# How x reaches the feed-forward layer's channel layout: TensorE transposes, or VectorE block transposes and a trip through memory

## The chip, the core and the metric

The kernel runs on one core of one Trainium2 chip. The metric is the device time of one execution in microseconds. Three runs of the kernel before gave 473.37, 473.84 and 475.94; the median is 473.84.

## What is computed

An mLSTM attention (4 sequences, 8 heads, 768 steps, 40 values a head) makes x of 3072 tokens by 320 channels, and a feed-forward layer (320 to 2048 to 320, with a leaky activation that has a slope of its own for each hidden channel) makes the output of it:

```
m_new = max(f + m, i);  C = exp(f + m - m_new) C + exp(i - m_new) v k^T;  n likewise with k
x = sigmoid(o) * (C q) / max(|n q|, 1)          # 8 heads of 40 side by side: 320 channels
h = x @ w_in;  g = max(h, 0) + alpha * min(h, 0);  out = g @ w_out
```

## The kernel before

The attention is done in its chunked form. A chunk is 128 tokens (n = 0 to 23), with tokens on the partitions; a group g is two chunks (256 tokens), and there are twelve groups (0 to 11). Chunks 0 to 5 (`NDIR = 6`), that is groups 0 to 2, are done in an opening whose order is written out by hand in `ORDER`. From group 3 on one string, `PATTERN`, is unrolled once a group: a name such as `xn.-1` is a step of chunk 2g-1, `X:-1` a step on x of group g-1, `V0<<` an up-step of the feed-forward layer of group g-2. Every engine runs its instructions in exactly the order in which the unrolled names issue them (`pin`), and an engine that waits holds up all that stands behind it. SyncE (SP) issues nearly all DMAs, in the same way: one queue, in order. The DMAs take turns on eight semaphores, so that one waits for the landing of the one issued eight before it.

**x by token.** `gated_steps` (L399) normalizes one chunk: reciprocal of the denominator, times the gate, times the numerator into the tile `xn` (L420, VectorE, 128 tokens by 320 channels). GpSimd then copies channels 256 to 319 a second time behind them (L424), since the third block of channels is used twice, once for each half of `W2`.

**x by channel.** The feed-forward layer's first matmuls need channels on the partitions. `x_steps` (L576) takes two PSUM tiles, has TensorE transpose the six blocks of 128 by 128 (`x_by_channel`, L551), and then splits the result into a rounded part and its rest for exactness: ScalarE copies to `XH` (L565) and `X2` (L568), VectorE subtracts to `XL` (L570) and `X2L` (L573). In `PATTERN` these are X (transposes), xa and xb (the two copies), xd and xe (the two subtractions).

**The feed-forward layer.** A group's eight up-steps (`up_steps`, L687) make 256 hidden channels each by 16 matmuls into a PSUM tile `ph` (L697 to L704; two such tiles take turns), then Relu on ScalarE (L707), the activation's other half on VectorE (L712), a rounded copy `gh` on ScalarE (L721) and the rest `gl` on GpSimd or VectorE (L723). Eight down-steps (L734) of 12 matmuls add up the output, which VectorE copies out (L767). V0 and U0 are the first up-step of a group; V0 is the first reader of the group's `XH` and `XL`.

**Other work on SP that stands close to x.** Two crossbar transposes a chunk bring q and k to channels (L269), four copies shift them (`shifted`, L279 to L282, the first two wait for the crossbar's landing), `state` sends the attention's state to its places (L233, L234, L236), `load_L` brings 512 KB of decays (L119), and `load_gate` (L128) brings six chunks of the output gate, once a sequence. The scratch tile that `state` sends from (tag `qf`) is one of two that `token_parts` also uses (L260), so the second of its GpSimd subtractions waits for the landing of L233 and L234.

Of the kernel before, what the change touches and what calls it, by code (L numbers as in the profile page):

```python
# [8 lines left out]
F32 = mybir.dt.float32  # L9
F32R = mybir.dt.float32r  # L10
# [3 lines left out]
ALU = mybir.AluOpType  # L14
# [3 lines left out]
def kernel(ctx: ExitStack, tc: tile.TileContext, q, k, v, i_gate, f_gate, o_gate, w_in, w_out, alpha, out):  # L18
# [380 lines left out]
    def gated_steps(n, hv):  # L399
        b, c = divmod(n, NC)  # L400
        g, j = divmod(n, GC)
        if j == 0:
            xn_tiles[g] = sb.tile([P, GC, DM + KR], F32, tag="xn", name=f"xn{g}")
        xn = xn_tiles[g]
        r = sb.tile([P, H], F32, tag="r", name=f"r{n}")
        if 0 < c and n < NBF:
            nc.vector.scalar_tensor_tensor(r, hv[:, :, D], 2.0, hv[:, :, D + 1], ALU.max, ALU.max)
        else:
            nc.vector.tensor_scalar(r, hv[:, :, D], 2.0, None, ALU.max)
            nc.vector.tensor_tensor(r, r, hv[:, :, D + 1], ALU.max)  # L410
        nc.vector.reciprocal(r, r)
        yield
        sg = o_tiles[b][:, c]
        rb = r.unsqueeze(2).broadcast_to([P, H, D])
        if b == 0:
            nc.vector.scalar_tensor_tensor(out=sg, in0=sg, scalar=1.0, in1=rb, op0=ALU.add, op1=ALU.mult)
        else:
            nc.gpsimd.tensor_tensor(sg, sg, rb, ALU.mult)
        yield
        (nc.gpsimd if c > 0 and n in XNP else nc.vector).tensor_tensor(  # L420
            xn[:, j, :DM].rearrange("p (h d) -> p h d", d=D), hv[:, :, :D], sg, ALU.mult
        )
# [19 lines left out]
    def late_steps(n):  # L442

        b, c = divmod(n, NC)
        g, j = divmod(n, GC)
        E, pS, Es, got = {}, {}, [None, None], {}

        def decays(par):
            Lb = pre[n] if par == 0 else pre.pop(n)
            E[par] = decays_of(n, par, Lb)  # L450
            if par == 0:
                got["E3"] = late_pool.tile([P, 2, 512], BF16, tag="t", name=f"E3_{n}", bufs=3)
            parts = E[par].bitcast(BF16).rearrange("p (k s) -> p k s", k=2)
# [24 lines left out]
        def add():  # L478
            nc.vector.tensor_tensor(got["T"], got["T"], got["S"], ALU.add)

        def gate():
            got["g"] = gated_steps(n, got["T" if c > 0 else "S"])
            next(got["g"])

        def upd():
            got["u"] = update_steps(n)
            next(got["u"])

        def tok():
            got["t"] = token_parts(n)  # L490
            next(got["t"])

        def val():
            got["v"] = value_parts(n)
            next(got["v"])

        def nxt(k):
            return lambda: got.__setitem__("S", next(got[k]) or got.get("S"))

        st = {}  # L500
        if n >= NDIR + 2:
            st["ld"] = lambda: load_qk(n)
            if j == 0:
                st["lv"] = lambda: load_v(g)
            st["lL"] = lambda: pre.__setitem__(n, load_L(n))
            st["ta"] = tok
            for k in "bcdefghi":
                st["t" + k] = nxt("t")
        if n > NDIR:
            st["sh"] = lambda: shifted(n)  # L510
            st["va"] = val
            for k in "bcd":
                st["v" + k] = nxt("v")
# [24 lines left out]
        st["r"] = gate
        for k in ("og", "xn", "xp"):
            st[k] = nxt("g")  # L540
        return st

    def drain(it):
# [1 line left out]
            pass  # L545

    def x_by_channel(g, j, p1, p2, kts=range(3)):
        xn = xn_tiles[g]
        for kt in kts:
            dst = p1[:, kt * GT :] if kt < 2 else p2  # L550
            nc.tensor.transpose(dst[:, j * P : (j + 1) * P], xn[:, j, kt * P : (kt + 1) * P], ident)  # L551

    def x_tiles_of(g):
        XH = sb.tile([P, 2, GT], F32R, tag="XH", name=f"XH{g}")
        XL = sb.tile([P, 2, GT], F32R, tag="XL", name=f"XL{g}")
        X2 = sb.tile([P, GT], F32R, tag="X2", name=f"X2{g}")
        X2L = sb.tile([P, GT], F32R, tag="X2L", name=f"X2L{g}")
        return XH, XL, X2, X2L

    def split_steps(g, ts, p1, p2, whole=False):  # L560
        if g not in x_tiles:
# [33 lines left out]
    def first_stacks():  # L595
# [40 lines left out]
        U12 fm5 ft5 o5h sc51 wg51 v5 o7d R12 S12 ta5 D10 G11 K11 o6s o6x gr5 og3 gg5 G12 gx5 gg4 D11 K12 D12 i30h i30l  # L636
        gx4 U13 gp5 D02 tp0 do3 U06 o7s gp4 o5l o6j vp0 R13 tp1 g05 S13 G13 N05 K13 o7x o6h D13 vp1 o7j U07 tp2 tp3
        R06 S06 R07 x4 x5 xa5 xd5 D03 D04 D05 S07 o7h o7l G06 K06 o6l D06 xa4 xd4 G07 K07 D07 Z0"""
    PATTERN = """og.-1 ua.0 m1.0 V4<< tf.1 ub.0 vb.1 xn.-1 V5<< tg.1 g2<< m0.0 N2<< vc.1 c1.0 r4<< vb.0 d1.0 xp.-1 th.1 h1.0 ti.1 uc.0
        s4<< ud.0 D2<< ue.0 U6<< g4<< l1.0 g3<< N3<< uf.0 r5<< lG.-1 c0.0 vd.1 X:-1 vc.0 ua.1 lG.2 sh.1 ub.1 s5<< N4<<  # L640
        oa.0 R6<< d0.0 g5<< ug.0 h0.0 l0.0 uc.1 V7<< N5<< xa:-1 vd.0 D3<< D4<< D5<< S6<< ta.2 tb.2 xb:-1 uh.0 lL.2
        y0.0 xd:-1 pi.0 r7<< s7<< G6<< wd.2 tc.2 K6<< ob.0 xe:-1 q0.0 td.2 y1.0 F< q1.0 e0.1 te.2 V0< e1.1 tf.2 g7<<
        ud.1 s0.1 r0< s1.1 V1< m0.1 s0< ui.0 c0.1 tg.2 m1.1 ta.3 c1.1 pt.0 d0.1 N7<< ad.0 D6<< ld.4 V2< D7<< th.2 d1.1
        ue.1 g0< uf.1 tb.3 r1< h0.1 r.0 s1< V3< l0.1 og.0 ug.1 ti.2 uh.1 wd.3 tc.3 h1.1 lv.4 r2< e0.2 xn.0 sh.2 Z<<
        l1.1 td.3 ui.1 pi.1 g1< s2< y0.1 N0< ld.5 xp.0 pt.1 e1.2 q0.1 r3< N1< y1.1 D0< q1.1 D1< s0.2 s1.2 va.3 ad.1
# [258 lines left out]
    def first_group():  # L904
# [398 lines left out]
```

## Time and profile before

| | |
|---|---|
| three runs: lowest, median, highest | 473.37, 473.84, 475.94 us |
| span of the profiled execution, first to last instruction | 474.2 us |
| TensorE matmul busy | 467.8 us, 99% of the span |
| VectorE, ScalarE, GpSimd busy | 308.6, 314.8, 308.4 us (65%, 66%, 65%) |
| x transposes on TensorE (L551) | 72, in 12 groups of six |
| DMA traffic | 61.61 MB, mean 130 GB/s |

The profiled execution has no time of its own beside its span; the span and the runs agree within 0.1% at the median. Times in rows are counted from the start of the span. PE is TensorE's matmuls, PEld its weight loads, DVE is VectorE, ACT ScalarE, POOL GpSimd, SPq the queue of SyncE. Matmuls overlap in the pipeline, so the row of one is longer than the distance to the next one's start.

### The profile page before, as it was taken

What the parts mean: (1) busy time and instruction counts of PE and PEld (TensorE: products, weight loads), DVE (VectorE), ACT (ScalarE), POOL (GpSimd) and SP (SyncE); (2) the same over time, 40 slices, a digit from 0 to 9 for tenths busy, and PEclk for the clock granted to TensorE, in tenths of its full rate; (3) what the DMA queues carried; (4) which work ended last, traced back from release to release, by engine and by line L of the source; (5) the groups of instructions that cost most, each with busy time, mean ns of one, the idle gap of its engine ahead of it and who ended that gap; (6) DMA issues with size and microseconds to landing.
All of it is one profiled execution on the core that took longest, in us unless ns stands there. A gap on an engine that the chain in (4) does not pass through costs nothing.

```text
span 474.2 us, 11834 instructions
## 1 busy us (share of the span) xinstructions
PE 467.8 (99%) x4442; PEld 454.9 (96%) x4442; DVE 308.6 (65%) x664; ACT 314.8 (66%) x716; POOL 308.4 (65%) x395
## 2 busy tenths in 40 slices
PE   8999999999999999999999999999999999999997
PEld 6899989999999999999999999999999999999997
DVE  3768988757776676676676676676676676663321
ACT  4969888766858659558658659558658658424322
POOL 8531674864788688578788688578788686334231
PEclk9959999999999999999999999999999999999999
DMA  9978994968784665768963784699784442000000
GB/s 186 207 175 225 267 217 121 209 130 167 160 156 116 133 150 117 129 150 174 148 148 108 111 169 117 126 148 184 147 129 114 94 113 61 1 28 1 29 2 28
DMA packets 173923, 61.61 MB, mean 130 GB/s; under 512 B 140154, under 2 KB 166122, under 8 KB 173866
## 3 DMA queue, kind: packets, MB, share of 16 engines
q1 hardware_dynamic: 173786, 60.75, 61.3%
q8 instruction: 35, 0.57, 0.6%
q14 instruction: 22, 0.18, 0.1%
q10 hardware_dynamic: 80, 0.11, 0.1%
HBM read 36.90 MB, written 4.03 MB: 86 GB/s over the span
## 4 chain that ended last, share of the span: by engine, by line
PE 89%; DVE 5%; POOL 2%; ACT 2%; issue 1%; POOLq 0%; DVEq 0%; ACTq 0%
PE po L734 35%; PE ph L697 5%; PE ph L703 4%; PE ph L700 4%; PE ph L698 4%; PE ph L699 4%; PE ph L702 4%; PE ph L704 4%; PE ph L701 4%; PE pH L361 4%; PE pS L462 3%; PE pH L322 2%; PE p L551 2%; PE pu L183 2%; PE pS L1033 1%; PE pI L386 1%
## 5 line engine op out<-in xcount | busy, mean ns | idle before, releaser
L723 POOL TENSOR_TENSOR gl<-g,gh 128x512 fp32r<-128x512 f32 x77 | 100.2, 1303 | 41.2 <-ACT gh L721 34.2
L734 PE MATMUL po<-OH,gh 128*128 128x320 f32 x368 | 110.7, 312 | 0.0
L734 PE MATMUL po<-OL,gh 128*128 128x320 f32 x368 | 109.4, 309 | 0.0
L707 ACT ACTIVATE g<-ph 128x512 f32<-128x512 f32 x96 | 57.2, 597 | 75.9 <-PE ph L704 71.8
L712 DVE SCALAR_TENSOR_TENSOR g<-g,oma,ph 128x256 f32<-128x256 f32 x156 | 67.0, 471 | 36.1 <-ACT g L707 36.0
L734 PEld LDWEIGHTS po<-OL,gh 128*128 128x128 f32 x368 | 69.2, 188 | 0.1
L734 PEld LDWEIGHTS po<-OH,gh 128*128 128x128 f32 x368 | 69.1, 188 | 0.0
L734 PE MATMUL po<-OH,gl 128*128 128x320 f32 x368 | 69.0, 309 | 0.0
L697 PE MATMUL ph<-XH,WH 128*128 128x256 f32 x192 | 58.0, 302 | 0.7 <-ACT wo L803 0.7
L734 PEld LDWEIGHTS po<-OH,gl 128*128 128x128 f32 x368 | 57.9, 188 | 0.0
L703 PE MATMUL ph<-XL,WH 128*128 128x256 f32 x192 | 54.2, 282 | 0.0
L700 PE MATMUL ph<-XH,WL 128*128 128x256 f32 x192 | 54.2, 282 | 0.0
L702 PE MATMUL ph<-XL,WH 128*128 128x256 f32 x192 | 54.2, 282 | 0.0
L698 PE MATMUL ph<-XH,WH 128*128 128x256 f32 x192 | 54.1, 282 | 0.0
L699 PE MATMUL ph<-XH,WL 128*128 128x256 f32 x192 | 54.1, 282 | 0.0
L701 PE MATMUL ph<-X,W 128*128 128x256 f32 x192 | 53.5, 279 | 0.3 <-POOL W L829 0.3
L704 PE MATMUL ph<-X2L,W 128*128 128x256 f32 x192 | 53.4, 278 | 0.0
L348 ACT CAST E<-pS 128x512 bf16<-128x512 f32 x72 | 41.1, 581 | 15.9 <-DVE pS L345 15.3
L721 ACT CAST gh<-g 128x512 fp32r<-128x512 f32 x77 | 46.5, 618 | 7.2 <-DVE g L712 4.8
L433 ACT ACTIVATE E<-Lb,bT 128x128 f32<-128x128 f32 x160 | 50.0, 391 | 0.0
L345 DVE TENSOR_TENSOR pS<-pS,E 128x512 f32<-128x512 f32 x36 | 25.0, 696 | 31.1 <-PE pS L462 27.5
L436 POOL TENSOR_SCALAR_AFFINE_SELECT E<-E 128x512 f32<-128x512 f32 x40 | 25.7, 642 | 22.6 <-ACT E L433 22.2
(193 smaller groups left out, 1142.7 us busy)
## 6 DMA issues: line engine op xcount, KB each, us to landing
Lb<-L_d SPq DMA_DIRECT2D x20, 512.0 KB
wo<-in_moe_w_out_dram SPq DMA_DIRECT2D x8, 640.0 KB
wi<-in_moe_w_in_dram SPq DMA_DIRECT2D x8, 512.0 KB
qn<-in_q_dram SPq DMA_DIRECT2D x24, 160.0 KB
kn<-in_k_dram SPq DMA_DIRECT2D x24, 160.0 KB
va<-in_v_dram SPq DMA_DIRECT2D x24, 160.0 KB
og<-in_o_gate_dram SPq DMA_DIRECT2D x24, 160.0 KB
out_dram<-ob SPq DMA_DIRECT2D x11, 320.0 KB
```

Source lines behind the costliest of these rows:

```text
L697: nc.tensor.matmul(dst, WH[half][:, 0, hs], XH[:, 0], start=True, stop=False)
L698: nc.tensor.matmul(dst, WH[half][:, 1, hs], XH[:, 1], start=False, stop=False)
L699: nc.tensor.matmul(dst, WL[half][:, 0, hs], XH[:, 0], start=False, stop=False)
L700: nc.tensor.matmul(dst, WL[half][:, 1, hs], XH[:, 1], start=False, stop=False)
L701: nc.tensor.matmul(dst, W2[:, fs], X2, start=False, stop=False)
L702: nc.tensor.matmul(dst, WH[half][:, 0, hs], XL[:, 0], start=False, stop=False)
L703: nc.tensor.matmul(dst, WH[half][:, 1, hs], XL[:, 1], start=False, stop=False)
L704: nc.tensor.matmul(dst, W2[:, fs], X2L, start=False, stop=True)
L707: nc.scalar.activation(gt, ph, AF.Relu, scale=-1.0)
L712: nc.vector.scalar_tensor_tensor(out=y[:, e], in0=gt[:, e], scalar=oma[:, f : f + 1], in1=ph[:, e], op0=ALU.mult, op1=ALU.add)
L723: (nc.vector if split else nc.gpsimd).tensor_tensor(gl, y, gh.bitcast(F32), ALU.subtract)
L734: nc.tensor.matmul(po[j], x[:, e, j * P : (j + 1) * P], W[f // NB][:, f % NB], **ends)
```

## The change

For chunks 6 to 23 (groups 3 to 11) TensorE's transposes are gone. VectorE transposes each square of 32 by 32 of `xn` in place of its position (two instructions a chunk, the second makes the doubled channels as well, so that GpSimd's copy is gone too). SP writes the result to a tile in memory, and once both chunks of a group are there it reads it back with four DMAs, one for each set of 32 partitions, so that the squares lie where a full transpose would have put them. ScalarE and VectorE then do the split from SBUF, one instruction each. Groups 0 to 2 keep TensorE's transposes; their `xn` tiles now have one buffer for even and one for odd chunks.

```diff
+    x_d = dram.tile([2, GC, P, 3 * P], F32, tag="x_d", name="x_d")
...
-        nc.gpsimd.tensor_copy(xn[:, j, DM:], xn[:, j, 2 * P : DM])
-        yield
+        if n >= NDIR:
+            by_blocks(n)
+        else:
+            nc.gpsimd.tensor_copy(xn[:, DM:], xn[:, 2 * P : DM])
+        yield
+
+    def by_blocks(n):
+
+        xn = xn_tiles.pop(n)
+        xt = sb.tile([P, P // 32, 3, 32], F32, tag="xt", name=f"xt{n}", bufs=1)
+        nc.vector.transpose(
+            xt[:, :, :2].rearrange("p m k b -> p k m b"), xn[:, : 2 * P].rearrange("p (k m b) -> p k m b", k=2, b=32)
+        )
+        nc.vector.transpose(
+            xt[:, :, 2].rearrange("p (d e) b -> p d e b", d=2),
+            xn[:, 2 * P :].rearrange("p (e b) -> p e b", b=32).unsqueeze(1).broadcast_to([P, 2, KR // 32, 32]),
+        )
+        xt_tiles[n] = xt
+
+    def blocks_out(n):
+
+        nc.sync.dma_start(x_d[n // GC % 2, n % GC], xt_tiles.pop(n).rearrange("p m k b -> p (m k b)"))
+
+    def blocks_in(g):
+
+        xr = sb.tile([P, GC * (P // 32), 3, 32], F32, tag="xr", name=f"xr{g}", bufs=1)
+        for m in range(P // 32):
+            nc.sync.dma_start(
+                xr[32 * m : 32 * (m + 1)].rearrange("a q k b -> a q (k b)"),
+                x_d[g % 2, :, :, 96 * m : 96 * (m + 1)].rearrange("j (i a) w -> a (j i) w", a=32),
+            )
+        return xr
...
     def x_steps(g):
-        p1, p2 = psa(f"p1_{g}"), psa(f"p2_{g}")
-        for j in reversed(range(GC)):
-            x_by_channel(g, j, p1, p2, (2, 0, 1))
-        yield
-        yield from split_steps(g, slice(0, GT), p1, p2, True)
-
+        xr = blocks_in(g)
+        yield
+        x_tiles[g] = XH, XL, X2, X2L = x_tiles_of(g)
+
+        def as_blocks(x):
+            return x.rearrange("p k (q b) -> p q k b", b=32)
+
+        nc.scalar.copy(as_blocks(whole_of[g][0]), xr)
+        yield
+        nc.vector.tensor_tensor(as_blocks(whole_of[g][1]), xr, as_blocks(whole_of[g][0].bitcast(F32)), ALU.subtract)
+        yield
```

In `PATTERN` xp (now the block transposes) stands right behind xn, xw (the write) is new, X (now the reads) stands behind the shifts sh.1 and ahead of the gate's load lG, xb and xe are gone, and the gate's opening (oa on ScalarE, ob on VectorE) comes some steps later, as its load does.

The order on three engines in group 7 (names of tiles carry buffer numbers; the line numbers of the changed kernel are higher: L280 to L283 are the shifts, L234 and L235 the state, L742 to L749 the up-step's matmuls, L452 the write, L458 the reads, L623 the subtraction to `XL`, L757 and L768 the activation's half and the rest `gl`). TensorE, between two up-steps of group 6, before:

```order
L703 MATMUL ph_6_4594<-XL_4064,WH_709 128x256
L704 MATMUL ph_6_4594<-X2L_4066,W_73 128x256
L551 MATMUL p_7_4625<-ident,xn_4326 128x128
L551 MATMUL p_7_4624<-ident,xn_4326 128x128 x2
L551 MATMUL p_7_4625<-ident,xn_4326 128x128
L551 MATMUL p_7_4624<-ident,xn_4326 128x128 x2
L697 MATMUL ph_7_4650<-XH_4063,WH_709 128x256
```

and in the changed kernel:

```order
L748 MATMUL ph_6_4599<-XL_4110,WH_709 128x256
L749 MATMUL ph_6_4599<-XL_4110,W_73 128x256
L742 MATMUL ph_7_4651<-XH_4109,WH_709 128x256
L743 MATMUL ph_7_4651<-XH_4109,WH_709 128x256
L744 MATMUL ph_7_4651<-XH_4109,WL_710 128x256
```

The six transposes are gone and nothing stands in their place; the rest of TensorE's order is the same. SyncE's queue from the crossbar transposes of an odd chunk on, before:

```order
L269 DMA_TRANSPOSE qS_4570<-Z_4261 128x8x128
L269 DMA_TRANSPOSE kS_4573<-Z_4261 128x8x128
L279 DMA qS_4570<-qS_4570 80x1024
L280 DMA kS_4573<-kS_4573 80x1024
L281 DMA qS_4570<-qS_4570 40x1024
L282 DMA kS_4573<-kS_4573 40x1024
L233 DMA C_87<-cw_4579 40x336
L234 DMA C_87<-cw_4579 40x2x336
L119 DMA Lb_4721<-L_d 128x8x128
L236 DMA C_87<-C_87 40x336
```

and in the changed kernel:

```order
L270 DMA_TRANSPOSE qS_4574<-Z_4259 128x8x128
L270 DMA_TRANSPOSE kS_4577<-Z_4259 128x8x128
L452 DMA x_d<-xt_4542 128x384
L280 DMA qS_4574<-qS_4574 80x1024
L281 DMA kS_4577<-kS_4577 80x1024
L282 DMA qS_4574<-qS_4574 40x1024
L283 DMA kS_4577<-kS_4577 40x1024
L458 DMA xr_4634<-x_d 32x8x96 x4
L234 DMA C_87<-cw_4584 40x336
L235 DMA C_87<-cw_4584 40x2x336
L120 DMA Lb_4719<-L_d 128x8x128
L237 DMA C_87<-C_87 40x336
```

One write stands ahead of the shifts, four reads ahead of the state; the even chunk's write stands alone elsewhere. VectorE around the split, before:

```order
L350 TENSOR_TENSOR E_16_4370<-pS_0_4474,E_0_4364 128x512
L712 SCALAR_TENSOR_TENSOR ph_6_4594<-g_6_4641,oma,ph_6_4594 128x256 x2
L570 TENSOR_TENSOR XL_4669<-p_7_4624,XH_4668 128x512
L712 SCALAR_TENSOR_TENSOR g_7_4755<-g_7_4755,oma,ph_7_4650 128x256 x2
L723 TENSOR_TENSOR gl_6_4760<-ph_6_4594,gh_6_4759 128x512
L136 TENSOR_SCALAR og_3398<-og_3398 128x640
L573 TENSOR_TENSOR X2L_4671<-p_7_4625,X_4670 128x256
```

and in the changed kernel:

```order
L351 TENSOR_TENSOR E_16_4368<-pS_0_4475,E_0_4362 128x512
L757 SCALAR_TENSOR_TENSOR ph_6_4599<-g_6_4642,oma,ph_6_4599 128x256 x2
L623 TENSOR_TENSOR XL_4715<-xr_4634,XH_4714 128x8x3x32
L757 SCALAR_TENSOR_TENSOR g_7_4753<-g_7_4753,oma,ph_7_4651 128x256 x2
L768 TENSOR_TENSOR gl_6_4758<-ph_6_4599,gh_6_4757 128x512
```

The one subtraction to `XL` stands where the larger of the two stood, ahead of the last two steps that read the up-steps' PSUM tiles `ph_6` and `ph_7` (L712 and L723); the smaller one and the gate's step are gone from here.

## Rows read from the trace of the kernel before

**Rows 1.** The page's first part: busy time, share and count of each engine.
```profile
PE 467.8 (99%) x4442; PEld 454.9 (96%) x4442; DVE 308.6 (65%) x664; ACT 314.8 (66%) x716; POOL 308.4 (65%) x395
```

**Rows 2.** Windows, two groups' periods: length, busy time by engine, clock, DMA share, GB/s.
```profile
251.10:286.80 35.70, 35.70 (x374) 35.05 (x374) 24.51 (x54) 25.01 (x60) 27.85 (x36) 1.00 0.66 130
286.80:322.30 35.50, 35.50 (x362) 35.06 (x361) 23.86 (x52) 24.61 (x58) 25.51 (x33) 1.00 0.72 135
```

**Rows 3.** Waits of PE in the whole run: total us, times, longest us.
```profile
PE warm L153 <- POOL ident masks.py:199: 1.4, 1, 1.4
PE ph L697 <- ACT wo L803: 0.7, 1, 0.7
```

**Rows 4.** Line 551 alone: ns least, median, most, first and last start.
```profile
L551 PE MATMUL p<-ident,xn x72: 270/272/274, 35.1 to 430.7; 128*128 128x128 f32 x72
```

**Rows 5.** Timeline of PE around group 7's transposes: start us, length us, what.
```profile
288.68 0.28 PE L704 MATMUL ph<-X2L,W 128*128 128x256 f32 x1
...
288.91 0.28 PE L698 MATMUL ph<-XH,WH 128*128 128x256 f32 x1
...
289.63 0.28 PE L704 MATMUL ph<-X2L,W 128*128 128x256 f32 x1
289.75 0.82 PE L551 MATMUL p<-ident,xn 128*128 128x128 f32 x6
...
290.52 0.29 PE L698 MATMUL ph<-XH,WH 128*128 128x256 f32 x1
```

**Rows 6.** Timeline of VectorE in group 7: the odd chunk's x, then the split.
```profile
282.56 0.48 DVE L420 TENSOR_TENSOR xn<-pI,og 128x320 f32<-128x320 f32 x1
...
293.75 0.86 DVE L712 SCALAR_TENSOR_TENSOR g<-g,oma,ph 128x256 f32<-128x256 f32 x2
294.53 0.69 DVE L723 TENSOR_TENSOR gl<-ph,gh 128x512 fp32r<-128x512 f32 x1
```

**Rows 7.** Timeline of PE: the first reader of group 7's x.
```profile
298.93 0.36 PE L697 MATMUL ph<-XH,WH 128*128 128x256 f32 x1
```

**Rows 8.** Groups of instructions by line and form: busy us, mean ns of one, idle before.
```profile
L767 DVE COPY ob<-po 128x320 f32<-128x320 f32 x22 | 9.8, 486 | 18.4 <-PE po L734 18.4
...
L829 DVE TENSOR_TENSOR OL<-t_wo,OH 128x640 fp32r<-128x640 f32 x8 | 7.0, 890 | 0.0
...
L825 ACT CAST OH<-t_wo 128x640 fp32r<-128x640 f32 x8 | 5.8, 727 | 0.0
```

**Rows 9.** Timeline of SP in group 7: issues, with the queue's own time for each.
```profile
282.43 1.23 SPq L269 DMA_TRANSPOSE kS<-Z  x1
...
285.51 0.54 SPq L280 DMA_DIRECT2D kS<-kS  x1
...
287.77 0.72 SPq L233 DMA_DIRECT2D C<-cw  x1
288.54 0.82 SPq L234 DMA_DIRECT2D C<-cw  x1
```

**Rows 10.** What DMAs take: waits of SP; timelines of SP and ACT at the start.
```profile
SPq L1298 <- DMA out_dram<-ob: 1.4, 1, 1.4
...
1.27 0.41 SPq L783 DMA_DIRECT2D wi<-in_moe_w_in_dram  x1
...
5.54 0.68 ACT L793 ACTIVATE t_wi<-wi 128x512 f32<-128x512 f32 x1 [2.53 <-DMA wi<-in_moe_w_in_dram]
```

**Rows 11.** Timeline of ScalarE in group 7: the last step ahead of x's copy.
```profile
292.32 0.48 ACT L256 CAST Z<-kn 128x320 bf16<-128x320 f32 x1
```

**Rows 12.** Timelines of SP (gate loads, group 8) and GpSimd (groups 7 and 8).
```profile
318.34 4.87 SPq L128 DMA_DIRECT2D og<-in_o_gate_dram  x6
...
327.19 0.81 SPq L234 DMA_DIRECT2D C<-cw  x1
...
294.81 0.79 POOL L260 TENSOR_TENSOR kr<-kn,Z 128x320 f32<-128x320 f32 x1
...
330.79 0.80 POOL L260 TENSOR_TENSOR kr<-kn,Z 128x320 f32<-128x320 f32 x1
```

More of the change, by code (lines that the diff above doesn't have):

```diff
@@ L401, in gated_steps @@
         g, j = divmod(n, GC)
-        if j == 0:
-            xn_tiles[g] = sb.tile([P, GC, DM + KR], F32, tag="xn", name=f"xn{g}")
-        xn = xn_tiles[g]
+        if n >= NDIR:
+            xn = sb.tile([P, DM], F32, tag="xn", name=f"xn{n}")
+        elif j == 0:
+            xn = sb.tile([P, GC * (P // 32), 3, 32], F32, tag="xr", name=f"xn{n}", bufs=1)
+            xn = xn.rearrange("p q k b -> p (q k b)")[:, : DM + KR]
+        else:
+            xn = sb.tile([P, P // 32, 3, 32], F32, tag="xt", name=f"xn{n}", bufs=1)
+            xn = xn.rearrange("p q k b -> p (q k b)")
+        xn_tiles[n] = xn
         r = sb.tile([P, H], F32, tag="r", name=f"r{n}")
@@ L420, in gated_steps @@
         (nc.gpsimd if c > 0 and n in XNP else nc.vector).tensor_tensor(
-            xn[:, j, :DM].rearrange("p (h d) -> p h d", d=D), hv[:, :, :D], sg, ALU.mult
+            xn[:, :DM].rearrange("p (h d) -> p h d", d=D), hv[:, :, :D], sg, ALU.mult
         )
         yield
-        nc.gpsimd.tensor_copy(xn[:, j, DM:], xn[:, j, 2 * P : DM])
+        if n >= NDIR:
+            by_blocks(n)
+        else:
+            nc.gpsimd.tensor_copy(xn[:, DM:], xn[:, 2 * P : DM])
         yield
+    def by_blocks(n):
[19 more added lines that the diff above has]
+        return xr
     def decays_of(n, par, Lb):
@@ L540, in late_steps @@
             st[k] = nxt("g")
+        st["xw"] = lambda: blocks_out(n)
         return st
@@ L547, in x_by_channel @@
     def x_by_channel(g, j, p1, p2, kts=range(3)):
-        xn = xn_tiles[g]
+        xn = xn_tiles.pop(g * GC + j)
         for kt in kts:
             dst = p1[:, kt * GT :] if kt < 2 else p2
-            nc.tensor.transpose(dst[:, j * P : (j + 1) * P], xn[:, j, kt * P : (kt + 1) * P], ident)
+            nc.tensor.transpose(dst[:, j * P : (j + 1) * P], xn[:, kt * P : (kt + 1) * P], ident)
     def x_tiles_of(g):
[L554 to L558, printed above, removed]
+        H = sb.tile([P, 3, GT], F32R, tag="XH", name=f"XH{g}")
+        L = sb.tile([P, 3, GT], F32R, tag="XL", name=f"XL{g}")
+        whole_of[g] = H, L
+        return H[:, :2], L[:, :2], H[:, 2], L[:, 2]
     def split_steps(g, ts, p1, p2, whole=False):
@@ L576, in x_steps @@
     def x_steps(g):
-        p1, p2 = psa(f"p1_{g}"), psa(f"p2_{g}")
-        for j in reversed(range(GC)):
-            x_by_channel(g, j, p1, p2, (2, 0, 1))
+        xr = blocks_in(g)
         yield
-        yield from split_steps(g, slice(0, GT), p1, p2, True)
+        x_tiles[g] = XH, XL, X2, X2L = x_tiles_of(g)
[5 more added lines that the diff above has]
+        yield
+    whole_of = {}
+    xt_tiles = {}
     chunk, xn_tiles, x_tiles, pre, vbs = {}, {}, {}, {}, {}
@@ L638 @@
         R06 S06 R07 x4 x5 xa5 xd5 D03 D04 D05 S07 o7h o7l G06 K06 o6l D06 xa4 xd4 G07 K07 D07 Z0"""
[L639 to L645, printed above, removed]
+    PATTERN = """og.-1 ua.0 m1.0 V4<< tf.1 ub.0 vb.1 xn.-1 xp.-1 V5<< tg.1 g2<< m0.0 N2<< vc.1 c1.0 r4<< vb.0 d1.0 th.1 h1.0 ti.1 xw.-1 uc.0
+        s4<< ud.0 D2<< ue.0 U6<< g4<< l1.0 g3<< N3<< uf.0 r5<< c0.0 vd.1 vc.0 ua.1 sh.1 X:-1 lG.-1 lG.2 ub.1 s5<< N4<<
+        R6<< d0.0 g5<< ug.0 h0.0 l0.0 uc.1 V7<< N5<< vd.0 D3<< D4<< D5<< S6<< ta.2 tb.2 xa:-1 uh.0 lL.2
+        y0.0 xd:-1 pi.0 r7<< s7<< G6<< wd.2 tc.2 K6<< q0.0 td.2 y1.0 F< q1.0 e0.1 te.2 V0< e1.1 oa.0 tf.2 g7<<
+        ud.1 s0.1 r0< s1.1 V1< m0.1 s0< ui.0 c0.1 tg.2 m1.1 ob.0 ta.3 c1.1 pt.0 d0.1 N7<< ad.0 D6<< ld.4 V2< D7<< th.2 d1.1
+        ue.1 g0< uf.1 tb.3 r1< h0.1 r.0 s1< V3< l0.1 og.0 ug.1 ti.2 uh.1 wd.3 tc.3 h1.1 lv.4 r2< e0.2 xn.0 xp.0 sh.2 xw.0 Z<<
+        l1.1 td.3 ui.1 pi.1 g1< s2< y0.1 N0< ld.5 pt.1 e1.2 q0.1 r3< N1< y1.1 D0< q1.1 D1< s0.2 s1.2 va.3 ad.1
         va.2 lL.3 te.3 r.1 s3<"""
@@ L1258, in first_group @@
         for g in range(2, NG):
-            add(f"X:{g} xa:{g} xb:{g} xd:{g} xe:{g}", lazily(lambda g=g: x_steps(g)))
+            add(f"X:{g} xa:{g} xd:{g}", lazily(lambda g=g: x_steps(g)))
         for name in in_full():
```

## The prediction

> **What bounds the kernel now.** First the busy shares: TensorE's matmuls fill 99% of the span, the other three compute engines about 65% each [rows 1]. A share is a mean over stages, so next the windows, cut by the period of one group. In both that are shown TensorE is busy for the whole length, 35.70 of 35.70 us and 35.50 of 35.50, at a granted clock of 1.00 (its upper level, 2.4 GHz), while VectorE, ScalarE and GpSimd have 8 to 12 us free in each [rows 2]. Then the waits, to see that a busy TensorE isn't one that waits inside: the whole run lists four of its waits, the longest 1.4 and 0.7 us, for things of the opening [rows 3]. So from the first hundred microseconds on the time is TensorE's instructions one after the other. What leaves its queue leaves the time, as long as nothing that it reads comes late.
>
> **What leaves TensorE.** 9 groups times 6 transposes, 54 of the 72. The row of one says 272 ns [rows 4], but neighbours overlap, so the price is read from starts. In group 7 the step from the last matmul of one half up-step (L704) to the second of the next (L698) takes 290.52 - 289.63 = 0.89 us with the six transposes in between, and 288.91 - 288.68 = 0.23 us one half earlier without them [rows 5]. The difference, 0.66 us or 0.11 a transpose, is what a group gains: 9 x 0.66 = 5.9 us. The bounds are narrow, since the same six stand between up-steps in every one of the nine groups.
>
> Against this stands a rule. The Trainium skill, "VectorE: DVE Perf Modes", sections "The three transpose paths" and "Rules for kernel authors", says to transpose 128x128 on TensorE if a PSUM destination will do, as VectorE transposes only within blocks of 32x32; its table has 390 ns for TensorE and 311 ns for VectorE (bf16). By 390 ns the 54 would be worth 21.1 us, as an estimate from that page; the rows give 5.9, because here a transpose follows another in a full pipeline. The rule's verdict, that this path is the dearer one, is the first rival below.
>
> **What is added, and what hides it.** I follow x of group 7 from the odd chunk's product to its first reader. The product ends at 282.56 + 0.48 = 283.0 [rows 6]; the first reader, V0, starts at 298.93 [rows 7] and, with the transposes gone from its own period, at 298.3. Everything new must fit into these 15.3 us.
>
> *Block transposes.* Two instructions of 256 and 128 elements a partition, which the trace doesn't have. A copy of 320 takes 486 ns [rows 8], so 384 at VectorE's rate are 0.6 us; at GpSimd's rate (0.80 us for 320 [rows 12]) they would be 1.0. I take 0.6, as the engine is VectorE; a gain is excluded, they are new there. They hold up only VectorE's next steps, and a group's 1.2 us go into its some 11 us of idle time [rows 2]. Done at 283.6.
>
> *The write.* SP is free of the crossbar transpose's issue at 282.43 + 1.23 = 283.7. The shift behind it (L280) waits until 285.51 for that transpose to land anyway [rows 9], so the write's issue is hidden there, and the shifts end at 287.7 as before, where L233 is issued now. How long does it take to land? The last output write ended SP's wait 1.4 us after its issue, about 2.0 with the issue; the crossbar transpose took 285.51 - 282.43 = 3.1; a 512 KB load in the opening 5.54 - 1.27 = 4.3 [rows 9, 10]. The write is 196 KB, in a period whose DMA engines are 0.7 busy [rows 2]: I take 3.1, with ends of 2.0 and 4.3. Landed at 286.8, before SP asks for it.
>
> *The reads.* Four issues of about 0.54 us [rows 9] from 287.7: the last is issued at 289.3 and lands, by the same 3.1, at 292.4. In exchange two copies on ScalarE become one of 768 elements: 727 ns for 640 [rows 8] make 0.87. It stands behind a step that ended at 292.8 [rows 11] and that now comes some 0.5 earlier, as `XH` used to be made ahead of it. So ScalarE waits 0.1 us: copy done at 293.3. The subtraction, 890 ns for 640 [rows 8], is 1.07: 294.4. Behind it on VectorE stand L712 and L723, 0.86 and 0.69 [rows 6], which free the PSUM tile that V0 writes: 295.9. That is 2.4 us ahead of V0's 298.3. With both ends against it (transposes 1.0, each trip 4.3) the same chain comes to 297.8, still 0.5 ahead. So x costs TensorE nothing, and if this cover is gone, V0 waits for VectorE's L723.
>
> *Behind the reads on SP.* The state's two DMAs (L233, L234) now follow four more issues, 2.2 us, and their readers on TensorE come most of a period later. But GpSimd's second subtraction (L260) reuses the buffer that L234 reads: L234 lands at 288.54 + 2.2 + 3.1 = 293.8 [rows 9], L260 starts at 294.81 [rows 12]: hidden by 1.0. Not so in groups 5 and 8, where the six gate loads (4.87 us) come in between: 327.19 + 2.2 + 0.5 for the write + 3.1 = 333.0 against 330.79 [rows 12], a wait of 2.2 us on GpSimd. Behind it stand the decays' masks and a `gl`, for which TensorE has no need for some microseconds; I take nothing for it and keep up to 2.2 for each of the two groups.
>
> *The rest.* GpSimd loses 18 small copies, off the path. The even chunk's write has half a period before its tile is written again. Later opening of the gate: its reader comes at the end of the period. Two PSUM tiles fewer a group in the rotation can only end waits sooner, and TensorE has none to lose.
>
> **Sum.** -5.9 + 0. The profiled span, 474.2, is 0.3 us (0.1%) above the median of 473.84, so the difference carries over: 473.84 - 5.9 = 467.9.
>
> **Rivals.**
> 1. *x comes late and the change is slower.* Price: the same chain with each trip at 5.0 us: write landed at 288.9, last read issued at 290.5 and landed at 295.5, then 0.87, 1.07, 0.86 and 0.69: 299.0, so V0 waits 0.7 us and the gain is gone: about 474. This is where it decides; each further 0.5 us on both trips adds 1.0 us to each of nine groups. At 5.5 us it is 1.7 x 9 - 5.9 = +9.4: 483. For it: four DMAs with short pieces, and DMA engines 0.7 busy [rows 2]. Against it: the big transfers that I see (decays, gate) are put behind the reads, and 512 KB took no more than 4.3 us. By the rule named above this is the likely case; the price of TensorE's transposes [rows 5] doesn't decide it, only the wait does.
> 2. *It cancels.* The trips near 5.0 us, or VectorE's or ScalarE's wait for x spreading into the up-steps' chain: 0.4 to 0.9 us a group given back, 472 to 476.
> 3. *Part is given back in groups 5 and 8*, by GpSimd's wait, in the middle of its bounds: 2 x 1.1 = 2.2, so 470.1.
>
> That the transposes don't leave TensorE is excluded by the order shown above.
>
> **Chances.** The forecast (467.2 to 469.2) 0.70: the bound engine is plain and the cover holds at both ends of every price. Rival 3: 0.12. Rival 2: 0.11. Rival 1: 0.07. What a measurement of this kernel can tell from no change is 0.5%, 2.4 us: faster is below 471.5, slower above 476.2. So faster is 0.70 + 0.12 = 0.82, same 0.11, slower 0.07. The range takes in the forecast and rival 3: 467.0 to 471.5, with 0.2 us under the forecast's own low end for the spread of the runs.
>
> **What would show it.** Right: TensorE's list of waits still has nothing after the opening, a group's period is 0.6 to 0.7 us shorter, the reads land ahead of ScalarE's copy or less than 1 us behind its turn, and V0 starts 1 us or more after L723's counterpart ends. Wrong: a wait of TensorE at V0 once a group, with ScalarE's copy waiting for the reads (rival 1, 2); GpSimd waiting for a DMA in groups 5 and 8 and TensorE for a `gl` behind it (rival 3); block transposes of several microseconds, which would push back VectorE's share of every up-step.

## The result and the profile after

The changed kernel takes 468.73 us (median of 6 runs, 465.72 to 470.18) against 473.61 us for the kernel before on the same chip (6 runs, 472.10 to 475.94). The ratio, estimated over all runs, is 0.9884, 95% interval 0.9851 to 0.9916; here and further down it isn't the quotient of the medians (0.9897 here). It is 4.9 us faster by medians and 5.5 by means (468.24 against 473.72); the forecast was 467.9 us, 5.9 less than before.

Runs of either kernel are spread over 4 to 5 us, because TensorE's granted clock falls for a few microseconds of the opening in some runs and not in others: from 25 to 30 us it was 0.50 in the profiled run of the changed kernel and 1.00 in a later profile of it. So kernels are best compared at equal mean clock of the run (34 runs of before and 18 of the changed kernel list it). At 0.996 the kernel before takes 473.55 us (mean of 9 runs) and the changed one 467.66 (2 runs): 5.9 less. At 0.989 it is 475.44 (15 runs) and 470.24 (5): 5.2 less. At 0.998 and above it is 471.86 (9) and 465.93 (4): 5.9 less. The profiled execution of the changed kernel took 470.16 us, 468.4 of them its span, at 0.989, the clock of the profiled one before it (span 474.2): 5.8 us less.

The page's busy times, which answer to [rows 1], and its line on memory traffic (36.90 MB read and 4.03 written before, so the trip adds 3.54 MB each way):

```profile
PE 461.9 (99%) x4388; PEld 449.2 (96%) x4388; DVE 334.1 (71%) x691; ACT 316.1 (67%) x707; POOL 308.4 (66%) x377
...
HBM read 40.44 MB, written 7.57 MB: 102 GB/s over the span
```

TensorE has 54 matmuls fewer and 5.9 us less to do. VectorE has 25.5 us more, of which the forecast's own prices (1.2 us of block transposes and nothing net for the split, in each of nine groups) make 10.8. That difference is followed below.

Two periods of the changed kernel by windows, cut at the first matmul of a group's first up-step, V0 (group 6 to 7, 7 to 8), with the columns of [rows 2]:

```profile
260.96:295.58 34.62, 34.62 (x358) 34.19 (x354) 27.18 (x56) 25.37 (x59) 27.24 (x34) 1.00 0.75 161
295.58:330.42 34.84, 34.84 (x357) 34.23 (x354) 27.18 (x59) 24.20 (x56) 25.37 (x31) 1.00 0.83 168
```

The same cut of the trace of before:

```profile
263.67:298.93 35.26, 35.26 (x363) 34.82 (x360) 23.83 (x52) 24.67 (x58) 27.21 (x36) 1.00 0.67 133
298.93:334.44 35.51, 35.51 (x364) 34.86 (x360) 24.13 (x55) 24.91 (x58) 25.76 (x33) 1.00 0.88 156
```

Each period is 0.64 and 0.67 us shorter, TensorE is busy through all of it as before, and VectorE has 3.0 to 3.4 us more to do. TensorE's waits over the whole run, which answer to [rows 3], are still four, all of the opening (the longest is shown; the others are 0.7, 0.4 and 0.2 us):

```profile
PE warm L154 <- POOL ident masks.py:199: 1.4, 1, 1.4
```

Where the six transposes stood [rows 5], one half of an up-step now follows the other as everywhere; further down the same timeline is V0 of group 7, which answers to [rows 7]:

```profile
286.93 0.28 PE L749 MATMUL ph<-XL,W 128*128 128x256 f32 x1
287.04 0.28 PE L742 MATMUL ph<-XH,WH 128*128 128x256 f32 x1
287.16 0.28 PE L743 MATMUL ph<-XH,WH 128*128 128x256 f32 x1
...
295.58 0.36 PE L742 MATMUL ph<-XH,WH 128*128 128x256 f32 x1
```

From L749 to the second matmul of the next half it is 287.16 - 286.93 = 0.23 us, where it was 0.89.

Now what hides the detour. VectorE's timeline in group 7, which answers to [rows 6] (start us, length us, what):

```profile
279.86 0.48 DVE L427 TENSOR_TENSOR xn<-pI,og 128x320 f32<-128x320 f32 x1
280.37 0.45 DVE L441 STREAM_TRANSPOSE xt<-xn 128x256 f32<-128x256 f32 x1
...
290.44 3.76 DVE L623 TENSOR_TENSOR XL<-xr,XH 128x768 fp32r<-128x768 f32 x1
294.13 0.86 DVE L757 SCALAR_TENSOR_TENSOR g<-g,oma,ph 128x256 f32<-128x256 f32 x2
294.91 0.68 DVE L768 TENSOR_TENSOR gl<-ph,gh 128x512 fp32r<-128x512 f32 x1
```

SyncE's queue in the same stretch, which answers to [rows 9]:

```profile
281.05 0.54 SPq L452 DMA_DIRECT2D x_d<-xt  x1
...
284.28 0.73 SPq L283 DMA_DIRECT2D kS<-kS  x1
285.12 1.90 SPq L458 DMA_DIRECT2D xr<-x_d  x4
```

And ScalarE's, which answers to [rows 11]; idle time of 0.2 us or more would stand in brackets behind a row:

```profile
289.14 0.47 ACT L257 CAST Z<-kn 128x320 bf16<-128x320 f32 x1
289.50 0.84 ACT L621 CAST XH<-xr 128x768 fp32r<-128x768 f32 x1
```

The reads are issued from 285.12, when the shifts are out of the way, until 287.02. ScalarE's copy of x starts at 289.50 without a wait, so they had landed within 2.5 us. Of the nine groups ScalarE waits for them in two (9 and 10), 1.0 us together; there they land 1.7 and 2.2 us after the last issue has ended. What was not foreseen stands in VectorE's row L623: the subtraction takes 3.76 us where 1.07 was taken. Over all groups, by line and form (busy us, mean ns, idle before):

```profile
L623 DVE TENSOR_TENSOR XL<-xr,XH 128x768 fp32r<-128x768 f32 x9 | 22.8, 2535 | 0.2 <-ACT XH L621 0.2
...
L261 POOL TENSOR_TENSOR kr<-kn,Z 128x320 f32<-128x320 f32 x18 | 16.5, 919 | 2.3 <-DMA C<-cw 2.1
...
L441 DVE STREAM_TRANSPOSE xt<-xn 128x256 f32<-128x256 f32 x18 | 8.0, 445 | 0.6
L444 DVE STREAM_TRANSPOSE xt<-xn 128x128 f32<-128x128 f32 x18 | 4.8, 269 | 0.0
```

The mean of 2.5 us hides a wide spread: the nine take 3.0, 3.7, 1.1, 3.0, 3.8, 2.3, 3.0, 1.4 and 1.5 us. VectorE's block transposes (12.8 us in all) and this one line (22.8) make 35.6 us; the two subtractions that it replaces took 0.68 and 0.41 in group 7, 9.8 in nine groups. The difference is 25.8, which accounts for VectorE's added 25.5. GpSimd's L261 for `kr`, 0.79 us for each before [rows 12], is at 0.92.

GpSimd's timeline beside the long subtraction of group 7:

```profile
290.25 0.79 POOL L339 TENSOR_TENSOR vb<-vr,vb 128x336 bf16<-128x336 f32 x1
...
291.13 0.81 POOL L261 TENSOR_TENSOR qr<-qn,Z 128x320 f32<-128x320 f32 x1
291.89 0.74 POOL L162 TENSOR_TENSOR kd<-kn,wT 128x320 f32<-128x320 f32 x1
292.57 0.82 POOL L261 TENSOR_TENSOR kr<-kn,Z 128x320 f32<-128x320 f32 x1
293.69 1.00 POOL L473 TENSOR_SCALAR_AFFINE_SELECT E<-E 128x512 f32<-128x512 f32 x1 [0.31 <-ACT E L470]
```

The subtraction's row begins at 290.44, while GpSimd is at L339, and ends at 294.20, 0.81 us after `kr` ends at 293.39. In group 5 it is the other way round. There the subtraction begins at 221.36 and ends at 222.50, 0.81 us after L339 ends at 221.69, and the `qr` that started meanwhile takes 1.37 (GpSimd's rows, then VectorE's):

```profile
220.91 0.78 POOL L339 TENSOR_TENSOR vb<-vr,vb 128x336 bf16<-128x336 f32 x1
...
221.78 1.37 POOL L261 TENSOR_TENSOR qr<-qn,Z 128x320 f32<-128x320 f32 x1
...
225.22 0.79 POOL L261 TENSOR_TENSOR kr<-kn,Z 128x320 f32<-128x320 f32 x1 [1.38 <-DMA C<-cw]
...
221.36 1.14 DVE L623 TENSOR_TENSOR XL<-xr,XH 128x768 fp32r<-128x768 f32 x1
```

The other groups fit in: in all nine the subtraction ends 0.81 or 0.82 us after the end of one of GpSimd's instructions, and its time goes by how many of them end between its start and that point (the `MEMSET` between them not counted): 3, 4, 1, 3, 4, 2, 3, 1 and 1.

This looks as if the two engines took turns. In these groups the subtraction is the one large instruction of VectorE whose operands both lie in SBUF, but for two products at the very end; in the kernel before, one of its operands lay in PSUM.

### The profile page after: what moved, and what is told of

Read it like the earlier page. It is cut to its first block, busy times and chain, and to the rows that moved or that the text cites. A ratio compares the mean times of both kernels' runs of the same rounds, so it can differ in the third digit from the quotient of the medians.

```text
span 468.4 us, 11843 instructions
## 1 busy us (share of the span) xinstructions
PE 461.9 (99%) x4388; PEld 449.2 (96%) x4388; DVE 334.1 (71%) x691; ACT 316.1 (67%) x707; POOL 308.4 (66%) x377
## 4 chain that ended last, share of the span: by engine, by line
PE 91%; DVE 5%; ACT 2%; issue 1%; POOL 0%; DVEq 0%; POOLq 0%; ACTq 0%
PE po L779 36%; PE ph L742 5%; PE ph L748 5%; PE ph L745 5%; PE ph L743 5%; PE ph L744 5%; PE ph L747 4%; PE ph L746 4%; PE ph L749 4%; PE pH L362 4%; PE pS L499 3%; PE pH L323 2%; PE pS L1078 2%; PE pu L184 2%; PE pI L387 1%; PE warm L154 1%
## 5 line engine op out<-in xcount | busy, mean ns | idle before, releaser
L768 POOL TENSOR_TENSOR gl<-g,gh 128x512 fp32r<-128x512 f32 x77 | 100.4, 1305 | 43.7 <-ACT gh L766 40.4
L757 DVE SCALAR_TENSOR_TENSOR g<-g,oma,ph 128x256 f32<-128x256 f32 x156 | 66.7, 468 | 32.7 <-ACT g L752 32.3
L742 PE MATMUL ph<-XH,WH 128*128 128x256 f32 x192 | 57.7, 300 | 0.7 <-ACT wo L848 0.7
L746 PE MATMUL ph<-XH,W 128*128 128x256 f32 x192 | 53.5, 278 | 0.2 <-POOL W L874 0.2
L749 PE MATMUL ph<-XL,W 128*128 128x256 f32 x192 | 53.4, 278 | 0.0
L742 PEld LDWEIGHTS ph<-XH,WH 128*128 128x128 f32 x192 | 36.1, 188 | 1.9 <-ACT wo L848 0.9
```

The costliest lines, as they stand in the source:

```text
L742: nc.tensor.matmul(dst, WH[half][:, 0, hs], XH[:, 0], start=True, stop=False)
L746: nc.tensor.matmul(dst, W2[:, fs], X2, start=False, stop=False)
L749: nc.tensor.matmul(dst, W2[:, fs], X2L, start=False, stop=True)
L757: nc.vector.scalar_tensor_tensor(out=y[:, e], in0=gt[:, e], scalar=oma[:, f : f + 1], in1=ph[:, e], op0=ALU.mult, op1=ALU.add)
L768: (nc.vector if split else nc.gpsimd).tensor_tensor(gl, y, gh.bitcast(F32), ALU.subtract)
```

## The experiments

**Theory A:** the gain is the six transposes a group and nothing else, as nothing that replaces them reaches TensorE while x comes early enough. **Theory B,** for VectorE's added time: its subtraction and GpSimd stand in each other's way. The rivals are in each expectation.

### The changed kernel, unchanged

> The changed kernel as it is, on the same chip as the next three. Theory A (the gain is the time of the 54 transposes on TensorE, and nothing waits in their place): 5 to 6.5 us below the kernel before, ratio 0.986 to 0.990, TensorE's waits as before. The single runs of the first measurement lay between 465.7 and 470.2, the mean granted clock between 0.999 and 0.988: I expect the same two ends again, and the same in the kernel before.

469.53 us (median of 6), ratio 0.9893, interval 0.9852 to 0.9934; span of the profiled run 466.2 us at clock 0.995. By medians this is 4.5 us less than the kernel before on this chip (473.99), under the 5 to 6.5 expected: four of the six runs had clock 0.988 or 0.989, but nine of the 23 of the kernel before. The ratio is as expected.

### The transposes put back beside the detour

```diff
         xr = blocks_in(g)
+        p1, p2 = psa(f"p1_{g}"), psa(f"p2_{g}")
+        for j in range(GC):
+            for dst in (p2, p1, p1[:, GT:]):
+                nc.tensor.transpose(dst[:, j * P : (j + 1) * P], ident, ident)
         yield
```

Nobody reads what these transposes write.

> The changed kernel with six transposes of the identity a group put back on TensorE, at the place of the old ones, into the same two PSUM tiles that nobody reads; the rest of the change stays. Theory A: each group is 0.66 us longer again, 9 x 0.66 = 5.9 us above the changed kernel, ratio to the kernel before 0.998 to 1.003. Rival B (the gain comes from what the change frees around TensorE: two PSUM tiles a group fewer or copies that GpSimd no longer makes): at least a part stays; if the PSUM tiles are not the cause but GpSimd's copies are, the time stays near the changed kernel's, ratio below 0.993.

473.10 us (median of 12), ratio 1.0004, interval 0.9975 to 1.0034: the kernel before, to the tenth of a per cent. At clock 0.996 it is 473.25 against 473.55. The windows of group 6 to 7 and 7 to 8, cut at V0:

```profile
261.54:296.80 35.26, 35.26 (x363) 34.82 (x360) 27.83 (x56) 25.54 (x59) 27.31 (x34) 1.00 0.71 155
296.80:332.26 35.46, 35.46 (x363) 34.85 (x360) 26.70 (x58) 24.27 (x56) 24.89 (x30) 1.00 0.81 168
```

The periods are those of before to within 0.05 us. VectorE still has 2.6 to 4.0 us more to do in each, and the trip through memory still runs. So all of the gain is the transposes' place on TensorE, and everything that the change adds costs it nothing. This run brings back the two PSUM tiles a group together with the transposes; the run with one operand in PSUM below takes the same two tiles without transposes and keeps the gain, so the tiles are not the cause.

### The reads later on SyncE's queue

```diff
-... ua.1 sh.1 X:-1 lG.-1 lG.2 ...
+... ua.1 sh.1 lG.-1 lG.2 ...
...
-... ta.2 tb.2 xa:-1 uh.0 lL.2
+... ta.2 tb.2 uh.0 lL.2 X:-1 xa:-1
```

> The four reads of a group are moved back on SyncE, behind the state's three transfers, the decays' 512 KB and, in groups 5 and 8, the gate's six loads; nothing else changes. In the changed kernel the last subtraction that frees V0's PSUM tile ends within 0.02 us of V0's start in groups 4 and 7, though the prediction reckoned 2.4 us of cover. Reads land some 3.5 us later (5 to 8 us later with gate loads). Theory A with the cover as the trace shows it: TensorE waits for V0 in every group, 1.5 to 3.5 us in seven and 5 to 8 us in two: 20 to 40 us above the changed kernel. With the cover as predicted: 1 us in seven and 4 in two: some 15 us. Rival (x is not what V0 would wait for, other work hides it): within 3 us of the changed kernel.

490.31 us (median of 4), ratio 1.0351, interval 1.0290 to 1.0412. From the profiled run, timelines in group 7, one after the other: of SyncE (the decays' load, the reads behind it), ScalarE, VectorE, TensorE and GpSimd, with the idle time before a row and what ended it in brackets.

```profile
298.05 0.49 SPq L120 DMA_DIRECT2D Lb<-L_d  x1
298.59 2.09 SPq L458 DMA_DIRECT2D xr<-x_d  x4
...
305.70 0.83 ACT L621 CAST XH<-xr 128x768 fp32r<-128x768 f32 x1 [5.69 <-DMA xr<-x_d]
...
306.56 0.96 DVE L623 TENSOR_TENSOR XL<-xr,XH 128x768 fp32r<-128x768 f32 x1 [5.63 <-ACT XH L621]
307.44 0.87 DVE L757 SCALAR_TENSOR_TENSOR g<-g,oma,ph 128x256 f32<-128x256 f32 x2
308.22 0.68 DVE L768 TENSOR_TENSOR gl<-ph,gh 128x512 fp32r<-128x512 f32 x1
...
308.45 0.36 PE L742 MATMUL ph<-XH,WH 128*128 128x256 f32 x1 [2.32 <-DVE g L757]
...
309.11 0.64 POOL L473 TENSOR_SCALAR_AFFINE_SELECT E<-E 128x512 f32<-128x512 f32 x1 [5.34 <-ACT E L470]
```

What TensorE waited for over the run (total us, times, longest us), the one entry behind the opening:

```profile
PE ph L742 <- DVE g L757: 14.2, 4, 5.1
```

Four things are to be seen. Behind the decays' load the reads land 5.0 us after the last was issued (300.68 to 305.70), not 2.5; in groups 3 to 9 it is 3.3 to 5.0 us. In group 10, where no decays' load stands ahead of them, they land after 1.8. The kernel loses because x is late, and at V0, as the first rival said. V0 starts 0.14 us after L757 ends (308.31) and 0.45 before L768 ends (308.90), so L757 is what it waits for; it is 0.14 or 0.15 us in each of groups 3 to 9. And the subtraction, with GpSimd idle from 303.76 to 309.11, takes 0.96 us.

Not as expected, TensorE's wait shows in four of the nine groups (4, 5, 7 and 8) and not in all; the loss against the changed kernel on this chip, 20.8 us by medians, is at the low end of the 20 to 40. TensorE's listed waits are 14.2 us, but the span is 21.7 longer than that of the changed kernel's first profile (490.1 against 468.4), which has the same stretch at 0.50 in its opening. Part of the rest is the clock. The wait of 5.1 us ends at 234.15; windows around that (columns as in [rows 2]):

```profile
230.00:234.00 4.00, 0.00 (x0) 0.00 (x0) 1.74 (x4) 2.60 (x6) 0.00 (x0) 0.66 0.60 78
234.00:238.00 4.00, 3.85 (x19) 3.79 (x20) 1.78 (x4) 3.83 (x12) 3.03 (x6) 0.50 0.14 27
```

In the four microseconds behind the wait TensorE runs at 0.50, its lower level of 1.2 GHz, and gets 19 matmuls done. Behind the other three waits it falls too.

### The split's subtraction with one operand in PSUM

The changed kernel ran once more on the chip of this run and the next:

> The changed kernel on the same chip as the next two, as their yardstick. The ratio to before of 0.988 to 0.990 of its earlier runs should come again, with the same pattern in the split's subtraction (3.0, 3.7, 1.1, 3.0, 3.8, 2.3, 3.0, 1.4 and 1.5 us from group to group).

It took 469.54 us (median of 6), ratio 0.9892, interval 0.9853 to 0.9930; the subtraction's mean was 2.42 us, in the same pattern but for group 6 (2.1 in place of 3.0).

```diff
-        nc.scalar.copy(as_blocks(whole_of[g][0]), xr)
+        p1, p2 = psa(f"p1_{g}"), psa(f"p2_{g}")
+        q1 = p1.rearrange("p (q k b) -> p q k b", k=2, b=32)
+        q2 = p2[:, :GT].rearrange("p (q b) -> p q b", b=32)
+        hb, lb = as_blocks(whole_of[g][0]), as_blocks(whole_of[g][1])
+        nc.scalar.copy(hb, xr)
+        nc.scalar.copy(q1, xr[:, :, :2])
+        nc.scalar.copy(q2, xr[:, :, 2])
         yield
-        nc.vector.tensor_tensor(as_blocks(whole_of[g][1]), xr, as_blocks(whole_of[g][0].bitcast(F32)), ALU.subtract)
+        nc.vector.tensor_tensor(lb[:, :, :2], q1, hb[:, :, :2].bitcast(F32), ALU.subtract)
+        nc.vector.tensor_tensor(lb[:, :, 2], q2, hb[:, :, 2].bitcast(F32), ALU.subtract)
```

> ScalarE copies what the reads brought once more, in two pieces, to two tiles of PSUM, and VectorE subtracts from there, so that one operand of each subtraction lies in PSUM, as it did in the kernel before. Theory A (VectorE and GpSimd stand in each other's way where both operands of VectorE's instruction lie in SBUF): the two subtractions take about 0.7 and 0.4 us in every group, 1.1 together in place of the mean of 2.5, and GpSimd's subtraction of q's rest that took 1.36 us beside it in group 5 is back at 0.8. Rival B (the instruction is slow for its pattern of blocks of 32, or because it is long): the two together stay at 2 us or more and go up and down with the group as before. The time: ScalarE has about 1.0 us more to do ahead of the subtraction, which then ends 1.5 us earlier in the groups where it took 3.7 us and at the same time where it took 1.1; since TensorE waits in neither kernel behind the opening, the time stays within 1 us of the changed kernel by both theories.

The two lines alone (ns least, median, most; first and last start):

```profile
L629 DVE TENSOR_TENSOR XL<-p,XH x9: 683/691/692, 151.2 to 427.3; 128x512 fp32r<-128x512 f32 x9
...
L630 DVE TENSOR_TENSOR XL<-p,XH x9: 411/414/416, 151.8 to 427.9; 128x256 fp32r<-128x256 f32 x9
```

GpSimd's two lines that stood beside it, from the groups of instructions:

```profile
L261 POOL TENSOR_TENSOR qr<-qn,Z 128x320 f32<-128x320 f32 x18 | 14.6, 813 | 8.2 <-issue 7.5 <-ACT Z L257 0.7
L261 POOL TENSOR_TENSOR kr<-kn,Z 128x320 f32<-128x320 f32 x18 | 14.4, 797 | 4.3 <-DMA C<-cw 4.1
```

All nine are now alike, with the same blocks of 32 and the same elements in all: 1.1 us together, and `kr` is back at 0.80 us. That is theory B of this section (theory A of the expectation above), and not the pattern or the length. The time is 467.79 us (median of 6), ratio 0.9880, interval 0.9842 to 0.9918; at clock 0.996 it is 467.71 against 467.66. So 1.4 us a group saved on VectorE are worth nothing here, as its lateness cost nothing.

### Group 2 by blocks as well

```diff
-        if n >= NDIR:
+        if n >= NBLK:
...
+    NBLK = 4
...
-        gx4 U13 gp5 D02 tp0 do3 U06 o7s gp4 o5l ...
-        R06 S06 R07 x4 x5 xa5 xd5 D03 ... D06 xa4 xd4 G07 ...
+        gx4 U13 gp5 xw5 D02 tp0 do3 U06 o7s gp4 xw4 o5l ...
+        R06 S06 R07 X:2 D03 ... D06 xa:2 xd:2 G07 ...
```

> Blocks and the trip through memory for group 2 as well (chunks 4 and 5), whose transposes stand at 98 us, where TensorE is already never idle. Theory A: 0.66 us less than the changed kernel if x of group 2 is there in time (its first reader comes some 15 us later), which is 0.14% and not to be told apart by the times alone; the trace should show 4382 matmuls and a span 0.5 to 0.7 us shorter at the same granted clock. Rival: in the opening VectorE's two transposes wait for GpSimd's product and push weights' work back: no gain or up to 2 us lost.

475.30 us (median of 12), ratio 1.0014, interval 0.9986 to 1.0041: the whole gain of the other nine groups is gone. Both sides of the expectation missed: neither 0.66 us won nor up to 2 us lost to VectorE's transposes, but 5.8 lost against the changed kernel on this chip, at another place. From the profiled run, timelines of SyncE and ScalarE:

```profile
104.27 2.05 SPq L458 DMA_DIRECT2D xr<-x_d  x4
...
108.04 0.83 ACT L621 CAST XH<-xr 128x768 fp32r<-128x768 f32 x1 [6.82 <-DMA xr<-x_d]
```

TensorE's one new wait of more than 0.3 us, from its list:

```profile
PE po L780 <- ACT gh L767: 4.0, 1, 4.0
```

And the windows of that stretch:

```profile
105.00:110.00 5.00, 1.04 (x6) 0.78 (x5) 1.10 (x2) 1.96 (x5) 0.00 (x0) 0.84 0.44 97
110.00:115.00 5.00, 5.00 (x30) 4.80 (x29) 1.53 (x4) 2.53 (x8) 3.29 (x5) 0.50 0.10 29
```

The reads were issued at 104.27, behind the crossbar transposes of two chunks and the shifts of one. ScalarE stood 6.8 us at the copy of x, although x is wanted only at V0, 19.6 us later (127.62); the copy of a product of group 0 (`gh`) stood behind it, TensorE waited 4.0 us for that, and then ran at clock 0.50. The next run puts the reads ahead of the second chunk's crossbar transposes, and copy and subtraction later:

```diff
-... o7j U07 tp2 tp3
+... o7j U07 X:2 tp2 tp3
...
-... D06 xa4 xd4 G07 ...
+... D06 G07 ...
...
+                    if name == "N14":
+                        names += ["xa:2", "xd:2"]
```

> Group 2 by blocks too, as in the run that lost 6 us with it, but with its reads put ahead of the transposed DMAs of the following chunk on the queue of SyncE, and ScalarE's copy and VectorE's subtraction put some 9 us later, behind ScalarE's copy of the fourth scores of that stretch. Theory A (the loss came from ScalarE, which stood 6.8 us at the copy of x while the products of group 0 queued behind it): the only wait of TensorE behind the opening, 4.0 us there, is gone, no stretch at clock 0.5 follows it, and 6 further transposes are saved: 0.6 to 0.7 us less than the changed kernel's span at the same clock of the opening. Rival B (GpSimd's and VectorE's work for the blocks of chunks 4 and 5 disturbs the opening wherever it stands): a wait of 1 us or more stays in the waits of TensorE between 80 and 125 us, and the time is 1 us or more above the changed kernel's.

468.26 us (median of 6), ratio 0.9889, interval 0.9850 to 0.9928. The wait of 4.0 us and the stretch at 0.50 are gone, so the loss did come from ScalarE's standing at a copy whose data had not landed. The run brings the reads forward and puts the copy back at once; which of the two was needed it doesn't tell. But the 0.6 us expected on top didn't come: at clock 0.999 it is 466.48 us (2 runs) against 465.88 (2) of the changed kernel. From V0 of group 1 to V0 of group 2 it is 43.99 us against 43.95, although six transposes are gone. The profile shows where they come back. At two places of this stretch TensorE starts a down-step's matmul late, at 90.31 behind ScalarE's rounded copy (`gg`) and at 99.84 behind VectorE's low part of the weights (`OL`); the second is this:

```profile
99.36 0.31 PE L781 MATMUL po<-OH,gh 128*128 128x320 f32 x1
99.84 0.41 PE L781 MATMUL po<-OL,gh 128*128 128x320 f32 x1 [0.17 <-DVE OL L876]
```

By the distance of starts, the six transposes took 0.57 us in the changed kernel here; the other matmuls of the stretch take 0.61 us more than there, and the delays at these two places account for that. Neither delay is as long as the 1 us of rival B; that the added work in the opening makes these two steps late is likely, but not shown. As it stands, neither this version nor the one before it beats the changed kernel.

## Why the prediction was right

**The bound and the gain: right.** TensorE's queue was the time, and 0.66 us a group left it. The forecast said 5.9 us; the spans at equal clock differ by 5.8, the periods by 0.64 and 0.67, and putting the transposes back undoes all of it. The rule weighed there (Trainium skill, "VectorE: DVE Perf Modes", "Rules for kernel authors") holds for the engines' time, by this trace: two instructions of 445 and 269 ns for what TensorE did in three steps of 110. It doesn't hold for the kernel's time, as VectorE had the time to spare and TensorE hadn't.

**From the median: right by luck of its size.** The text put the profiled execution 0.3 us above the median by its span. But a run takes 1.8 us beyond its span (470.16 against 468.4), so that execution was at the upper end of the runs, at clock 0.989, and 2.1 us above their median. The difference of 5.9 carries over at equal clock all the same; the median of six runs, though, follows whichever clocks they drew. That accounts for the 0.8 us between 467.9 and 468.73.

**Block transposes:** 0.71 us a chunk where 0.6 was taken, inside the bounds.

**The trip: shorter than taken.** 3.1 us from the start of an issue to the landing was taken. Counted so, the reads landed within 2.9 us in group 7 and after 2.2 and 2.6 in the two groups where ScalarE waited for them. So x was ready ahead of ScalarE in group 7, and in seven of the nine groups.

**The subtraction: the step that failed.** Its 1.07 us were worked out from 890 ns for 640 elements [rows 8], as if its length alone set its time. It takes 1.1 to 3.8 us, mean 2.5. The row behind the 890 had the sign in it, as its least, median and most in the trace of before show:

```profile
L829 DVE TENSOR_TENSOR OL<-t_wo,OH x8: 773/818/1441, 40.9 to 103.1; 128x640 fp32r<-128x640 f32 x8
```

Seven of the eight took 0.77 to 0.82 us; the one of 1.44 began while GpSimd was at a product. With 0.96 us when GpSimd is idle, 0.68 and 0.41 with one operand in PSUM, and `qr` or `kr` stretched when it comes second, this is shown to be a contest of the two engines. The Trainium skill states it ("SBUF — State Buffer", "Who interferes with whom"): a VectorE instruction with two SBUF inputs contends with a GpSimd instruction that reads SBUF, and the one that comes second is held until the first is done. The trace agrees, but the first isn't all that there is to wait for: here VectorE was held for up to four GpSimd instructions in a row.

**The cover: smaller than forecast, and enough.** The 2.4 us ahead of V0 were reckoned to the end of L723, whose counterpart L768 ends at 295.59 in group 7, with V0's start at 295.58: nothing is left, where the prediction's sign for being right was 1 us or more. That sign was itself wrong. V0 doesn't wait for that instruction: the run with late reads shows it waiting for L757, the counterpart of L712. L757 ends at 294.99, so the cover is 0.6 us in group 7, the smallest of groups 3 to 10, and 0.14 of it is the distance that V0 keeps when it does wait. The subtraction's 2.7 us more used up all of the 2.4; what is left is the 0.6 us by which V0 waits for less than was thought.

**GpSimd in groups 5 and 8: smaller.** A wait of 2.2 us in each was forecast and taken as free. The trace has 2.1 us in two waits together, 1.38 in group 5 and 0.71 in group 8, and TensorE has none behind it. Rival 3 is out.

**Rival 1: the mechanism is real, the condition wasn't met.** Reads behind the decays' load, which are issued later and land 3.3 to 5.0 us after it, make V0 late and the kernel slower by 3.5%. The rival's own price, 5.0 us for each trip with the reads at their place, no run tries; its chain also has the write landed 0.2 us later than its terms give (283.7 + 5.0 = 288.7), so V0's wait in it would be 0.5 us and not 0.7. What the change hangs on is the reads' place ahead of the decays' load on SyncE.

## What to carry to other kernels

Where one engine is busy without a gap, price what leaves it by the distance of starts in its full queue, and everything on the other engines only by whether it arrives in time. Work that waits for a DMA on an in-order engine is to stand where its data has certainly landed, not where it could be first: one early copy held a foreign product back and cost as much as nine groups had gained. And before moving an operand from PSUM to SBUF, look at what GpSimd does beside the instruction.

## What was not expected of the hardware

- VectorE's subtraction of 768 elements from SBUF and SBUF took 0.96 us with GpSimd idle and up to 3.76 beside it. In all nine groups it ended 0.81 or 0.82 us after the end of one of GpSimd's instructions. Why it got in behind the first of them in group 5 and only behind the fourth in group 7, with the same instructions in the same order, no run here shows.
- The same four reads landed 1.7 to 2.2 us after their last issue with no decays' load ahead of them (the three places of the two profiles where ScalarE waited for such reads), and 3.3 to 5.0 us after it right behind that load (groups 3 to 9 of the run with late reads).
- A wait of 4 to 5 us of TensorE was followed by several microseconds at granted clock 0.50, so that it cost more than its length, in both kernels that had one. Windows of 4 us from 192 and from 308 us on in the run with late reads, behind waits of 1.8 and 2.3 us, are at 0.72 and 0.73 as well.
